# The gate and up gradients in DRAM: from rows of tokens to square blocks of one token tile and one f block

## The chip, the cores and the metric

The kernel runs on one core of a Trainium2 chip. The metric is the device time of one execution in microseconds (us). Of five runs of the kernel before, the median is 2046.41 us, the fastest 2044.51 and the slowest 2056.77.

The engines are named as the profile names them: PE multiplies matrices (PEld are its weight loads), DVE works on vectors, ACT on activations and copies, POOL and SP mostly issue DMAs here. PEq, SPq, ACTq and POOLq are the engines' instruction queues; each is in order, so an instruction that waits holds up all that stands behind it. The DMAs of all queues run on the same 16 DMA engines.

## The reference

The kernel computes a small network with its backward pass: a layer norm, a state-space convolution (A), a gated feed-forward block (B), their product, and the gradients of all inputs. There are L = 2048 tokens, D = 576 features, F = 4608 hidden features and N = 128 states. What matters here is the feed-forward block and its gradient:

```python
def _B_ref(x, w1, w3, w2):
    gate = jnp.einsum("bsd,df->bsf", x, w1)
    up = jnp.einsum("bsd,df->bsf", x, w3)
    h = _silu(gate) * up
    out = jnp.einsum("bsf,fd->bsd", h, w2)
    return out

xn = _layernorm(x)
s = _A_ref(xn, ...)
g = _silu(_B_ref(xn, w1, w3, w2))
out = x + s * g            # and jax.vjp of all this at grad_out
```

In the backward pass the gradient of `h` is formed first, then the gradients of gate and up (called gg and gu), all of shape 2048 x 4608. From these come the gradients of w1 and w3 (products with `xn` over the tokens) and the gradient of `xn` (products with w1 and w3 over f), which goes through the layer norm's own gradient into the gradient of x.

## The kernel before

Tokens are cut into LT = 16 tiles of 128, f into FT = 36 blocks of 128, and f also into 18 groups of FG = 256 (two blocks each). The kernel goes forward (up to some 800 us), then backward. In the backward part three streams of work interleave.

**The feed-forward gradient**, `phase6_group` (lines 1252 to 1281), once for each of 18 groups of f. `phase6_load` has loaded gate and up of this group from `GI_dram` into `gg_n` and `h_n`, and transposed rows of w2 into `w2T`. For four token tiles at a time PE forms the gradient of h (`ph`, line 1267), ACT copies it to `gh`, and DVE multiplies it into `gu_n` and `gg_n` (line 1273). Then `gu_n` and `gg_n`, each 128 tokens x 16 tiles x 256 f, are stored to `GU_dram` and `GG_dram` (line 1280) by four DMAs on SP's queue, and `phase6_grad13` (line 1314) forms the gradients of w1 and w3 from the same tiles on PE. `phase6_grad2` (line 1295) forms the gradient of w2.

**The convolution's gradient** (`ssm_bwd_conv`, mostly DVE) runs until about 1280 us; after it `param_quarter` (lines 1042 to 1075) loads transposed pieces of `Q_dram` into `qT` by SP's queue, and PE (line 1065) and DVE reduce them to the parameters' gradients, until about 1870. `phase5_final` then makes and stores the small parameter gradients (`gout`).

**The gradient of the input**, `phase6_inputs` (lines 1329 to 1363), once for each of 16 token tiles, from about 1650 to the end. `ggc` and `guc` (two buffers each) hold gg and gu of one token tile, transposed: f within a block on the partitions, then 36 blocks x 128 tokens. They are read from `GG_dram` and `GU_dram` by `nat_transpose` (line 1218), a DMA that transposes as it moves, on SP's queue. PE then makes 144 matmuls per token tile (line 1357) into two accumulators `px`, alternating between `ggc` and `guc` block by block, against transposed w1 and w3 kept in SBUF. DVE and ACT finish the tile through the layer norm's gradient (`ln_bwd_tile`).

The code names each step's due time with `self.at(us)`, which sets a priority; a planner orders each engine's queue by these priorities and by what is ready when it plays the program through at build time. So SP's queue holds stores of gg and gu, transposing loads of w2, w1, w3, Q, ggc and guc and plain loads, in one order fixed at build time, and instructions of the three streams stand between each other in it.

Before, `GG_dram` and `GU_dram` are [16 token tiles, 128 tokens, 4608 f]. A store takes eight token tiles (j = 0 or 1) of all 256 f of the group; in DRAM each token gets a run of 256 elements, 512 bytes. A load takes one token tile, [128 tokens, 4608 f], whose rows are 9,216 bytes apart.

Of the kernel before, what the change touches and what calls it, by code (L numbers as in the profile page):

```python
# [14 lines left out]
BF16 = mybir.dt.bfloat16  # L15
I32 = mybir.dt.int32
P = 128
# [42 lines left out]
class K:  # L60
# [1100 lines left out]
    def backward(self, T0, TG, TQ, TC, TX, gctx, mats):  # L1161
        nc, cfg = self.nc, self.cfg
        D, L, LT, F, FT = cfg.D, cfg.L, cfg.LT, cfg.F, cfg.FT
        self.GG_dram = self.dram.tile([LT, P, F], BF16, name="GG_dram")
        self.GU_dram = self.dram.tile([LT, P, F], BF16, name="GU_dram")
        self.GXN_dram = self.dram.tile([P, LT, D], FP32, name="GXN_dram")
        NG = F // self.FG
        T2 = T0 + TG * NG
        FA = 12
        pool = self.tc.tile_pool  # L1170
        PS = bass.MemoryType.PSUM
        with ExitStack() as out:
            ffn = ExitStack()
            wp = ffn.enter_context(pool(name="e_w", bufs=2))
            elp = ffn.enter_context(pool(name="e_el", bufs=3))
            gwp = ffn.enter_context(pool(name="e_gw", bufs=2))
            rowp = ffn.enter_context(pool(name="e_w2r", bufs=1))
            inp = ffn.enter_context(pool(name="e_in", bufs=2))
            self.at(T0 - TG)
            self.w2rows = [rowp.tile([P, cfg.DT * P], BF16, name=f"w2r{i}") for i in range(4)]  # L1180
            for w2r in self.w2rows:
                nc.gpsimd.memset(w2r[:, D:cfg.DT * P], 0.0)
            ps_h = ffn.enter_context(pool(name="e_ps_h", bufs=3, space=PS))
            ps_gw = ffn.enter_context(pool(name="e_ps_gw", bufs=2, space=PS))
            ps = out.enter_context(pool(name="b_ps", bufs=3, space=PS, side="right"))
            self.ssm_bwd_conv(T0, TQ, ps)
            mats.close()
            fix = out.enter_context(pool(name="b_fix", bufs=1, side="right"))
            S_all = fix.tile([P, 4, D], FP32, name="S_all")
            wA = out.enter_context(pool(name="x_wA", bufs=1, side="right"))  # L1190
            self.at(T2 - 150)
            wT = [self.load_wT(wA, 0, FA)]
            T1 = T0 + 4 * TQ
            self.ssm_bwd_params(T1, TC, S_all, ps)
            self.at(T1 + TC * D // 16)
            self.phase5_final(out, fix, S_all, ps)
            cur = self.phase6_load(0, T0 - TG, TG, wp, inp)
            for gi in range(NG):
                nxt = self.phase6_load(gi + 1, T0 + TG * gi, TG, wp, inp) if gi + 1 < NG else None
                self.at(T0 + TG * gi)  # L1200
                self.phase6_group(gi, cur, elp, gwp, ps_h, ps_gw)
                cur = nxt
            ffn.close()
            gctx.close()
            self.phase6_inputs(T2, TX, FA, wT)
# [46 lines left out]
    def phase6_group(self, gi, tiles, elp, gwp, ps_h, ps_gw):  # L1252
        nc, cfg = self.nc, self.cfg
        D, LT, FG = cfg.D, cfg.LT, self.FG
        nfull = D // P
        LH = LT // 2
        w2T, hn, gg, gu = tiles
        for s in range(LH // 2):
            gh = elp.tile([P, 2, 2, FG], BF16, name="gh6")
            ph = [ps_h.tile([P, 2, FG], FP32, name="ph") for _ in range(2)]  # L1260
            for k in range(2):
                for j in range(2):
                    tt = s * 4 + j * 2 + k
                    m, i = divmod(tt, self.cfg.KT)
                    steps = [(self.goT[m][:, c, i * P:(i + 1) * P], w2T[:, :, c, :]) for c in range(nfull + 1)]
                    for n, (lw, rh) in enumerate(steps):
                        nc.tensor.matmul(ph[j][:, k, :].rearrange("p (a f) -> p a f", f=P), lhsT=lw, rhs=rh, start=(n == 0),  # L1267
                                         stop=(n == nfull))
            for j in range(2):
                nc.scalar.copy(out=gh[:, j], in_=ph[j][:])  # L1270
            sl = slice(s * 4, s * 4 + 4)
            for t_ in (gu, gg):
                nc.vector.tensor_tensor(out=t_[:, sl], in0=gh[:].rearrange("p j t f -> p (j t) f"), in1=t_[:, sl],  # L1273
                                        op=ALU.mult)
            if s % 2 == 1:
                self.phase6_grad2(gi, s // 2, hn, gwp, ps_gw)
        for (dst, t_) in ((self.GU_dram, gu), (self.GG_dram, gg)):
            for j in range(2):
                ts = slice(j * LH, (j + 1) * LH)
                nc.sync.dma_start(out=dst[ts, :, gi * FG:(gi + 1) * FG].rearrange("t p f -> p t f"), in_=t_[:, ts, :])  # L1280
        self.phase6_grad13(gi, gg, gu, gwp, ps_gw)

    def phase6_grad2(self, gi, fl, hn, gwp, ps_gw):
# [45 lines left out]
    def phase6_inputs(self, T2, TX, FA, wT):  # L1329
        nc, cfg = self.nc, self.cfg  # L1330
        D, DT, L, LT, F, FT = cfg.D, cfg.DT, cfg.L, cfg.LT, cfg.F, cfg.FT
        aps = self.aps
        pieces = self.dpieces()
        with self.tc.tile_pool(name="x_wB", bufs=1) as wB, \
                self.tc.tile_pool(name="x_in", bufs=2) as inp, \
                self.tc.tile_pool(name="l_sb", bufs=2) as sb, self.tc.tile_pool(name="l_sm", bufs=4) as sm, \
                self.tc.tile_pool(name="x_ps", bufs=2, space=bass.MemoryType.PSUM) as ps:
            for i in range(LT):
                self.at(T2 + TX * i)
                if True:  # L1340
                    ggc = inp.tile([P, FT, P], BF16, name="ggc")
                    guc = inp.tile([P, FT, P], BF16, name="guc")
                    self.nat_transpose(ggc[:], self.GG_dram[i])
                    self.nat_transpose(guc[:], self.GU_dram[i])
                    if i == 0:
                        wT = wT + [self.load_wT(wB, FA, FT)]
                    px = [ps.tile([P, 512], FP32, name=f"px{pi_}") for pi_ in range(len(pieces))]
                    gx = sb.tile([P, D], FP32, name="gx7")
                    gxs = sb.tile([P, D], FP32, name="gxs7")
                    nc.scalar.dma_start(out=gxs[:], in_=self.GXN_dram[:, i, :])  # L1350
                    go_t = sb.tile([P, D], BF16, name="go7")
                    nc.scalar.dma_start(out=go_t[:], in_=aps["grad_out"].flatten_outer_dims()[i * P:(i + 1) * P, :])
                    for fi in range(FT):
                        part, f = (0, fi) if fi < FA else (1, fi - FA)
                        for ai, act in enumerate((ggc, guc)):
                            for pi_, (po, pw) in enumerate(pieces):
                                nc.tensor.matmul(px[pi_][:, 0:pw], lhsT=act[:, fi, :], rhs=wT[part][ai][:, f, po:po + pw],  # L1357
                                                 start=(fi == 0 and ai == 0), stop=(fi == FT - 1 and ai == 1))
                    for pi_, (po, pw) in enumerate(pieces):
                        nc.vector.tensor_tensor(out=gx[:, po:po + pw].rearrange("p (g d) -> p g d", g=4),  # L1360
                                                in0=px[pi_][:, 0:pw].rearrange("p (g d) -> p g d", g=4),
                                                in1=self.perm(gxs[:])[:, :, pi_, :], op=ALU.add)
                    self.ln_bwd_tile(sb, sm, gx, i, go_t)
# [119 lines left out]
```

## Time and profile before

| What | Value |
|---|---|
| Median of 5 runs | 2046.41 us |
| The profiled execution's own time | 2044.51 us |
| Its span, from the first to the last instruction | 2042.7 us |
| PE busy | 1754.6 us, 86% |
| DVE busy | 1284.5 us, 63% |
| ACT busy | 940.0 us, 46% |
| DMA queue of SP (q1) | 615,952 packets, 294.84 MB, 58.6% of 16 engines |
| GU_dram and GG_dram stores | 36 each of 512 KB, median 5.0 and 6.2 us from issue to landing |
| ggc and guc loads | 16 each, on SP's queue for 5.27 and 5.31 us (median), 8.8 and 8.6 us from issue to landing |

A row of a wait reads: engine and line that waited, the work that ended the wait, total us, how many times, the longest. A row of a timeline reads: start in us from the span's start, duration, engine, line, operation, output and input. The duration of a DMA's row on SPq is the time that its issue held the queue, not the transfer. A DMA view gives, for a stretch of time, the throughput in 40 equal slices, and for each queue the packets, megabytes and the time that its packets took as a share of 16 engines over that stretch. A windows row gives start:end, length, busy us (and instructions) of PE, PEld, DVE, ACT and POOL, then the clock granted to PE as a share of full speed, the DMA share and GB/s.

### The profile page before, as it was taken

Reading aid. Unit: us, or ns where it says so; the run is one execution under the profiler, and the core shown is the slowest. Engines: PE = TensorE matmul, PEld = TensorE weight load, DVE = VectorE, ACT = ScalarE, POOL = GpSimd, SP = SyncE. Lnnn points to the kernel's source line nnn. Section 1 sums busy time; section 2 is a strip of 40 time slices with the busy share of each in tenths; the row PEclk is TensorE's granted clock in tenths of the full one; section 3 lists DMA queues with packets and bytes.
Section 4 is the critical chain, followed back from the end, with each engine's and each line's share of the span. In section 5 each row is a group of like instructions: output and inputs, shape, how many; then the busy total and the mean of one; then the engine's idle time right before and its main releaser. Section 6 shows DMA issues by size and latency. Waiting matters only on the chain.

```text
span 2042.7 us, 39357 instructions
## 1 busy us (share of the span) xinstructions
PE 1754.6 (86%) x16104; PEld 1281.6 (63%) x16104; DVE 1284.5 (63%) x2646; ACT 940.0 (46%) x1512; POOL 273.0 (13%) x347
## 2 busy tenths in 40 slices
PE   3779999999699995999999999868888926889978
PEld 1444444443388874778888888657777815668756
DVE  9558888978287723696966979435465341445722
ACT  5658888887545534745445454334554200000000
POOL 4113333333322103000000000000000000000000
PEclk7889999999899997999999999979899957999989
DMA  4868999998956568465664646999999799999673
GB/s 130 279 269 304 365 375 376 368 358 316 306 138 179 141 142 261 113 195 179 188 203 127 208 124 204 195 236 223 233 229 237 151 217 217 234 198 200 125 160 87
DMA packets 681861, 448.92 MB, mean 220 GB/s; under 512 B 477136, under 2 KB 640848, under 8 KB 671952
## 3 DMA queue, kind: packets, MB, share of 16 engines
q1 hardware_dynamic: 615952, 294.84, 58.6%
q0 software_dynamic: 27952, 126.24, 17.3%
q10 hardware_dynamic: 37776, 25.32, 4.5%
q8 instruction: 126, 2.06, 0.4%
q14 instruction: 55, 0.45, 0.1%
HBM read 128.29 MB, written 206.88 MB: 164 GB/s over the span
## 4 chain that ended last, share of the span: by engine, by line
PE 31%; DVE 20%; DMA 11%; SPq 6%; ACT 3%; issue 2%; POOL 0%; ACTq 0%; DVEq 0%; POOLq 0%
PE px L1357 9%; PE pgw L1314 8%; SPq L1218 5%; PE po L873 4%; DMA qT<-Q_dram 3%; DVE cm_t L696 3%; PE ph L1267 3%; PE pgw L1295 2%; DVE cm_t L693 2%; DMA guc<-GU_dram 2%; DVE Z L694 2%; DVE Z L699 1%; DVE Z L698 1%; DMA gg_n<-GI_dram 1%; PE et_ps L715 1%
## 5 line engine op out<-in xcount | busy, mean ns | idle before, releaser
L808 PE MATMUL pgu<-wmB_w,xnT 128*128 128x512 bf16 x1152 | 284.8, 380 | 1.1 <-ACT E L447 1.1
L1357 PE MATMUL px<-wTB_w,guc 128*128 128x288 bf16 x1152 | 244.7, 294 | 42.4 <-DMA guc<-GU_dram 29.8
L1357 PE MATMUL px<-wTB_w,ggc 128*128 128x288 bf16 x1152 | 245.4, 294 | 30.5 <-DMA ggc<-GG_dram 12.9
L1314 PEld LDWEIGHTS <-xn_bf 128*128 128x128 bf16 x2304 | 226.0, 98 | 37.3 <-issue 9.5
L1070 DVE TENSOR_TENSOR pr_q<-et_ps,pz 128x512 f32<-128x512 f32 x144 | 93.9, 682 | 195.7 <-PE et_ps L1065 120.4
L1267 PE MATMUL ph<-w2T,goT 128*128 128x256 bf16 x1440 | 194.1, 287 | 1.9 <-DMA w2T<-w2r 1.0
L808 PEld LDWEIGHTS <-xnT 128*128 128x128 bf16 x1152 | 102.7, 97 | 124.1 <-issue 23.3
L1374 ACT ACTIVATE t<-gx 128x576 f32<-128x576 f32 x16 | 10.9, 683 | 355.7 <-DVE gx L1360 263.9
L1357 PEld LDWEIGHTS <-guc 128*128 128x128 bf16 x1152 | 114.9, 100 | 81.1 <-DMA guc<-GU_dram 34.8
L1295 PE MATMUL pgw<-go_o,h_n 128*128 128x288 bf16 x1152 | 157.4, 291 | 7.9 <-DVE h_n L1249 7.8
L1267 PEld LDWEIGHTS <-goT 128*128 128x128 bf16 x1440 | 143.5, 102 | 28.5 <-issue 2.0
L1357 PEld LDWEIGHTS <-ggc 128*128 128x128 bf16 x1152 | 114.9, 100 | 57.9 <-issue 12.3
L873 PE MATMUL po<-w2g,hc 128*128 128x288 bf16 x1152 | 148.3, 286 | 2.7 <-DMA hc<-H_dram 2.7
L1316 ACT CAST gw<-pgw 128x256 bf16<-128x256 f32 x144 | 53.5, 373 | 202.6 <-PE pgw L1314 195.3
L1295 PEld LDWEIGHTS <-h_n 128*128 128x128 bf16 x1152 | 113.2, 99 | 37.6 <-DVE h_n L1249 8.6
L1360 DVE TENSOR_TENSOR gx<-px,gxs 128x288 f32<-128x288 f32 x32 | 13.3, 451 | 195.9 <-PE px L1357 195.9
L1314 PE MATMUL pgw<-gg_n,xn_bf 128*128 128x256 bf16 x1152 | 131.1, 275 | 4.4 <-ACT gw L1316 4.4
L1314 PE MATMUL pgw<-gu_n,xn_bf 128*128 128x256 bf16 x1152 | 131.7, 272 | 2.5 <-DVE gu_n L1273 1.6
L873 PEld LDWEIGHTS <-hc 128*128 128x128 bf16 x1152 | 111.2, 98 | 30.2 <-DMA hc<-H_dram 3.2
L1270 ACT CAST gh<-ph 128x512 bf16<-128x512 f32 x144 | 80.4, 591 | 84.6 <-PE ph L1267 59.3
L813 ACT CAST gu_t<-pgu 128x1024 bf16<-128x1024 f32 x108 | 110.3, 1023 | 11.1 <-DMA GI_dram<-gu_t 11.1
L811 ACT ACTIVATE s_t<-pgu 128x512 bf16<-128x512 f32 x144 | 87.7, 611 | 39.5 <-PE pgu L810 38.7
(323 smaller groups left out, 3490.4 us busy)
## 6 DMA issues: line engine op xcount, KB each, us to landing
GI_dram<-gu_t POOLq DMA_DIRECT2D x72, 512.0 KB, 7.6
Q_dram<-q_k SPq DMA_DIRECT2D x36, 1024.0 KB, 6.9
E_dram<-E_k POOLq DMA_DIRECT2D x18, 1152.0 KB, 5.7
E_l<-E_dram SPq DMA_DIRECT2D x36, 576.0 KB, 8.4
H_dram<-h_t SPq DMA_DIRECT2D x72, 256.0 KB, 7.3
gg_n<-GI_dram POOLq DMA_DIRECT2D x18, 1024.0 KB, 5.8
h_n<-GI_dram POOLq DMA_DIRECT2D x18, 1024.0 KB, 8.5
GU_dram<-gu_n SPq DMA_DIRECT2D x36, 512.0 KB, 5.0
```

Source lines behind the costliest of these rows:

```text
L696: tt_(out=f(t2), in0=f(B)[:, :, ::-1], in1=Az.rearrange("p q k d -> p q (k d)")[:, :, None].to_broadcast([P, Q, 2, KT * Wq]), op=ALU.mult)
L808: nc.tensor.matmul(pgu[:, j], lhsT=xnT[:, c, ts], rhs=wm[w][:, c, :], start=(c == 0), stop=False)
L811: nc.scalar.activation(out=s_t[:, :, q, :], in_=pgu[:, 0].rearrange("p (g f) -> p g f", g=ng), func=ACT.Silu)
L813: cp(out=gu_t[:, :, :, q, :], in_=pgu[:].rearrange("p u (g f) -> p u g f", g=ng))
L873: nc.tensor.matmul(pos[k][:, pi_, 0:pw], lhsT=hcs[k][:, fi, :], rhs=w2[fi][:, po:po + pw], start=(fi == 0), stop=(fi == FT - 1))
L1070: nc.vector.tensor_tensor(out=pr[:, s].rearrange("p k r x -> p r k x"), in0=T[:], in1=pz[:, s:s + 2, h * 8:h * 8 + 8, :].rearrange("p r d ...
L1218: self.nc.sync.dma_start_transpose(out=dst, in_=src)
L1267: nc.tensor.matmul(ph[j][:, k, :].rearrange("p (a f) -> p a f", f=P), lhsT=lw, rhs=rh, start=(n == 0), stop=(n == nfull))
L1270: nc.scalar.copy(out=gh[:, j], in_=ph[j][:])
L1295: nc.tensor.matmul(pgw[pi_][:, 0:pw], lhsT=hn[:, tt, fl * P:(fl + 1) * P], rhs=go_o[:, tt, po:po + pw], start=(tt == 0), stop=(tt == LT - 1))
L1314: nc.tensor.matmul(pw_[:, 0:FG], lhsT=self.xn_bf[:, tt, c * P:(c + 1) * P], rhs=nat[:, tt, :], start=(tt == 0), stop=(tt == LT - 1))
L1357: nc.tensor.matmul(px[pi_][:, 0:pw], lhsT=act[:, fi, :], rhs=wT[part][ai][:, f, po:po + pw], start=(fi == 0 and ai == 0), stop=(fi == FT - ...
```

## The change

The two DRAM tensors become [16 token tiles, 36 f blocks, 128 tokens, 128 f]: for each token tile and each f block one block of 128 x 128 elements, 32 KB, that lies in one piece. Within a token tile the 36 blocks follow each other, so the whole tile is one piece of 1.18 MB.

The stores are split by f block instead of by halves of the tokens: still four DMAs of 512 KB a group on SP's queue, in the order GU, GU, GG, GG in the program, but each now carries one f block of all 16 token tiles, and the run of one token is 128 elements, 256 bytes.

The loads see their source as a matrix of 4,608 rows (36 blocks x 128 tokens) by 128 columns, with rows of 256 bytes that follow each other without a gap, instead of 128 rows by 4,608 columns. What arrives in `ggc` and `guc` is the same, and so is all that follows.

```diff
@@ backward
-        self.GG_dram = self.dram.tile([LT, P, F], BF16, name="GG_dram")
-        self.GU_dram = self.dram.tile([LT, P, F], BF16, name="GU_dram")
+        self.GG_dram = self.dram.tile([LT, FT, P, P], BF16, name="GG_dram")
+        self.GU_dram = self.dram.tile([LT, FT, P, P], BF16, name="GU_dram")
@@ phase6_group
         for (dst, t_) in ((self.GU_dram, gu), (self.GG_dram, gg)):
-            for j in range(2):
-                ts = slice(j * LH, (j + 1) * LH)
-                nc.sync.dma_start(out=dst[ts, :, gi * FG:(gi + 1) * FG].rearrange("t p f -> p t f"), in_=t_[:, ts, :])
+            for l in range(FG // P):
+                nc.sync.dma_start(out=dst[:, gi * FG // P + l].rearrange("t p f -> p t f"), in_=t_[:, :, l * P:(l + 1) * P])
         self.phase6_grad13(gi, gg, gu, gwp, ps_gw)
@@ phase6_inputs
-                    self.nat_transpose(ggc[:], self.GG_dram[i])
-                    self.nat_transpose(guc[:], self.GU_dram[i])
+                    self.nat_transpose(ggc[:].rearrange("p l t -> p (l t)"), self.GG_dram[i].rearrange("l t f -> (l t) f"))
+                    self.nat_transpose(guc[:].rearrange("p l t -> p (l t)"), self.GU_dram[i].rearrange("l t f -> (l t) f"))
```

## The prediction

> **What bounds the kernel now.** I read the whole-kernel page first, then the windows view, then who waited for whom in the two stretches where the changed tensors live, then SP's queue in order of time. The windows view (start:end, length, then busy us of each engine, granted clock, DMA share, GB/s) has these stretches:
>
> ```profile
> 820.00:1280.00 460.00, 433.90 (x4512) 370.98 (x4511) 369.58 (x770) 230.35 (x461) 21.54 (x40) 1.00 0.57 172
> 1280.00:1640.00 360.00, 297.78 (x3165) 251.33 (x3162) 177.91 (x256) 140.85 (x235) 10.72 (x20) 0.90 0.99 217
> 1800.00:1850.00 50.00, 42.19 (x418) 33.28 (x416) 21.20 (x35) 1.55 (x4) 0.00 (x0) 0.93 1.13 201
> ```
>
> The stores of the change fall in the first two stretches, the transposing loads from 1640 on. In the first, DMA is only 57% busy. In the other two it is full, so a change in what a DMA costs can reach the end of the kernel. What PE waits for, in 1280 to 1640 (first line) and in 1640 to the end (the others; columns are total us, times, longest):
>
> ```profile
> PE et_ps L1065 <- DMA qT<-Q_dram: 52.5, 7, 24.2
> ```
> ```profile
> PE px L1357 <- DMA guc<-GU_dram: 29.8, 6, 7.8
> PE px L1357 <- DMA wTB_w<-in_B_w_dram: 25.3, 4, 10.9
> PE px L1357 <- DMA ggc<-GG_dram: 12.9, 3, 8.3
> ```
>
> So 42.7 us of PE's waits, about 2% of the kernel, end with a transposing load of the changed tensors. They are what a faster load could win, and the end is not all theirs: the chain of waits has one unbroken piece of PE px L1357 from 1963.33, 72.30 us long. The last four token tiles run at PE's own pace of 18 us, with loads that take 11 us of SP's queue per tile.
>
> **The loads: 16 of ggc and 16 of guc.** Each moves 36 blocks of 128x128, before and after. One transposing load of the same shape stands alone in the trace: hc from H_dram, laid out like GG_dram before. This is the DMA view of 610.7 to 617.0:
>
> ```profile
> GB/s 0 0 0 104 0 0 0 0 5 78 111 128 138 179 215 232 293 293 291 291 286 289 293 289 291 291 289 289 289 289 294 289 291 286 289 293 293 350 273 181
> q1 hardware_dynamic: 4640, 1.18, 83.6%
> ```
>
> 4,640 packets for 1.18 MB are 4,608 of 256 bytes (one row of one block each) and 32 of 4 bytes. 83.6% of 16 engines for 6.3 us over 4,640 packets is 18.2 ns per packet; in the packet records themselves the 10th, 50th and 90th percentiles are all 18 ns. The rate while it runs is 290 GB/s, 4.07 us for the 1.18 MB. The question is whether contiguous source rows make the packets larger or quicker. Two rows speak against it. The w2T loads, whose source rows lie in SBUF and not in DRAM, have the same 18 ns median; so the stride of 9,216 bytes between DRAM rows is not what a packet waits for. And a block is still 128 rows of 256 bytes each, spread over 16 engines. No load in this trace has a contiguous source, so the cost is bounded from both sides. The Trainium skill, "DMA: Bandwidth & Descriptors", section "Latency and other measured facts", gives a DMA transpose 261 GB/s with a non-contiguous middle dimension and some 350-400 GB/s when contiguous. By that rule (375 taken, an estimate) a load takes 3.15 us, 0.92 less. SP issues 16 of them between 1702.6 and 1864, where its queue has hardly a gap, and two more at 1945.9 and 1952.1 in front of PE's last wait: 18 x 0.92 = 16.5 us won at most, 2028. But the trace has 290, not 261, for the strided form, and packets without a tail. I take 0 and keep -16.5. On the other side, 16 neighbouring rows read at once could meet in the same part of the memory; with nothing in the trace to size it I allow 0.6 us a load, 18 x 0.6 = +11.
>
> **The stores: 72 before, 72 after, 512 KB each.** Before, a store writes runs of 512 bytes (one token, 256 f); after, runs of 256 bytes: 2,048 packets in place of 1,024. The first fence is a GU and a GG store before, alone, in 950.5 to 955.6; the second the small parameter stores (gout, 256-byte rows, SBUF to DRAM as the new stores are) in 1886.2 to 1889.2:
>
> ```profile
> q1 hardware_dynamic: 2080, 1.05, 67.2%
> ```
> ```profile
> q10 hardware_dynamic: 225, 0.05, 9.0%
> ```
>
> 67.2% x 5.1 us x 16 / 2,080 = 26.4 ns for 512 bytes; 9.0% x 3 us x 16 / 225 = 19.2 ns for 256 bytes. Per engine a store costs 64 x 26.4 = 1.7 us (1.8 at 290 GB/s), after the change 128 x 19.2 = 2.46 us if packets don't overlap, and 1.8 us, no more than before, if they overlap as in the hc load. I take 2.46: +0.65 us a store, +2.6 us for the four of a group, 47 us of engine time in all. The skill speaks against the change here: the same page, section "Specifications", wants at least 512 bytes and says that below it the engine reads, modifies and writes. If that doubles a byte's price, a 256-byte packet costs 28 ns, a store 3.6 us, +7.2 us a group. The row says 19.2, and I go by the row; 7.2 stays as the upper end.
>
> **What covers it.** Groups 0 to 8 end before 1280, where DVE sets the pace and DMA is 57% busy. Exposed there is only DVE's wait for the landing of GXN_dram stores on the same queue (10.5 us in 4 waits): 1 us, estimated from that. From 1340 each group does the same; SP's queue in one of them:
>
> ```profile
> 1363.03 0.54 SPq L1280 DMA_DIRECT2D GU_dram<-gu_n  x1
> 1363.67 0.57 SPq L1280 DMA_DIRECT2D GG_dram<-gg_n  x1
> 1364.34 2.02 SPq L1280 DMA_DIRECT2D GU_dram<-gu_n  x1
> 1366.45 1.38 SPq L1280 DMA_DIRECT2D GG_dram<-gg_n  x1
> 1367.92 7.47 SPq L1218 DMA_TRANSPOSE w2T<-w2r  x1
> 1381.01 12.32 SPq L1218 DMA_TRANSPOSE qT<-Q_dram  x3
> ```
>
> The w2T load, 1.2 us elsewhere, holds SP for 7.47 because four stores are ahead of it on the engines. It ends at 1375.4, and the qT loads that PE waits for next are issued at 1381.0, when PE has freed their buffers after 16 us of grad13. So 5.6 us of cover. The other groups by the same reading have 4.4 (1419.2 to 1423.6), 7.1, 6.3, 5.5, and 14 in the last two. Against it stand the 2.6 us and up to 1.3 us from order: a store used to carry eight token tiles and the first could go once half of them were multiplied; a block column has all sixteen, so the first pair waits for the last multiplication (1363.0 against 1364.3 here). 3.9 us is under 4.4: nothing shows. If the cover were gone all seven groups would pay, 27 us. The one group without cover is that of 1300: there PE waits 24.2 us for qT, behind SP's stores and ten weight loads in a row (1312.6 to 1340.9). It pays 2.6. On SP, what stands behind a store that waits longer is w2T and qT, whose readers are ph (a group later) and et_ps; POOL's loads of gg_n and h_n have their own queue and share only the engines. The last store is issued at 1617.7 and lands in about 6 us; the first ggc load is issued at 1647.5, so the store's new shape delays no load.
>
> **Sum.** Loads 0, early groups +1, the 1300 group +2.6, later groups 0: +3.6 on the profiled execution's own 2044.5 (span 2042.7 and 1.8 around it) is 2048.1. The median of the runs is 1.9 above that execution; the forecast as a median is 2050.
>
> **Rivals.** First, contiguous reads are quicker (the skill's 350-400): 2028 on the profile, 2030 as a median. For it: 42.7 us of PE waits to take from, a DMA share above 1. Against it: 18 ns whether rows come from DRAM or SBUF. Second, slower: 256-byte writes are dear. The place is the burst at the end of a group, the cover 4.4 to 7.1 us. It begins to cost once the burst grows by 3 us (with the 1.3 of order), which is 0.75 us a store or 20 ns a packet, and it passes +10 at about 25 ns. At 28 ns: 7.2 + 1.3 = 8.5 us against covers of 5.6, 4.4, 7.1, 6.3, 5.5 loses 13.6, with 7.2 at 1300 and some 3 early: +24, 2070. If the packets were twice as slow as 19.2, 38 ns, the burst grows by 12.2: 8 x 5 groups and 12 at 1300, +55, 2100. Third, the order on SP's queue comes out differently, since the planner that lays the queues out sees other stores. Whether qT or guc stands first decides waits of 6.6 to 7.8 us (tiles 1, 4 and 6). Two or three such waits more or fewer: 2030 to 2072, more easily worse, since the due times were set for the old order; slow loads (+11) are put with it.
>
> **Chances.** The loads unchanged and the stores covered: 0.50, with its own range 2042 to 2058. Quicker loads 0.14. Dear stores 0.18. Another order or slower loads 0.18. Faster by over 0.5% (10 us, about what a measurement of this kernel can tell from no change): 0.11 of the second and 0.03 of the fourth, 0.14. Slower by over 0.5%: 0.17 of the third, 0.12 of the fourth, 0.06 of the first, 0.35. The rest, 0.51, within. The range leaves out the better half of the quick loads and the tail of the dear stores: 2033 to 2080.
>
> **What would show it.** In the profile after, one load of ggc alone should again have 4,608 packets of 256 bytes at 18 ns and hold SP for 4.5 to 5.3 us; GU and GG stores should have 2,048 packets at 18 to 20 ns; the w2T load behind a burst should end before the qT loads' buffers come free; PE's waits for guc and ggc should stay near 43 us. I am wrong if the load's packets change size or rate, if the wait of et_ps for qT grows by more than 5 us between 1340 and 1640, or if the order of ggc, guc and qT on SP's queue differs.

## The result and the profile after

Run side by side on one chip, the changed kernel takes 2067.05 us (median) and the kernel before 2055.58 us: a ratio of 1.0050, with a 95% interval of 1.0034 to 1.0066. The ratio leaves out executions in the chip's slower state, so it is not quite the ratio of the two medians. The forecast was +3.6 us, a ratio of 1.0018. What came is about +10 us, at the edge of what the prediction counted as no change, and on the slower side. On the 2046.41 us of the first five runs it is 2056.6, inside the range of 2033 to 2080. The profiled execution of the changed kernel takes 2064.16 us with a span of 2062.4, against 2044.51 and 2042.7 before. Lines of the file beyond the stores have moved up by one, so L1357 is now L1356, and so on.

The windows view of the changed kernel, in the same stretches, shifted by 20 us where the later start needs it (columns as before):

```profile
820.00:1280.00 460.00, 432.95 (x4472) 369.32 (x4471) 364.91 (x759) 224.63 (x456) 20.48 (x38) 0.99 0.59 170
1280.00:1660.00 380.00, 301.04 (x3217) 253.72 (x3214) 181.79 (x263) 143.58 (x238) 10.72 (x20) 0.90 1.02 207
1820.00:1870.00 50.00, 44.00 (x427) 34.25 (x423) 24.19 (x42) 2.02 (x6) 0.00 (x0) 0.93 1.05 208
```

The middle row has the loss. Its stretch was taken 20 us longer, and still PE is busy for only 301 us of it instead of 298, while the DMA engines move 207 GB/s where they moved 217, although they are busy for as large a share. (Counted from one point of the work to another, this stage takes 337.0 us instead of 321.8; the two rows stand under the table further down.) PE's waits in 1280 to 1658 of the changed kernel (engine, line and what ended the wait: total us, times, longest):

```profile
PE et_ps L1065 <- DMA qT<-Q_dram: 42.5, 7, 12.4
PE ph L1267 <- ACT gh L1270: 16.3, 3, 8.6
PE pgw L1313 <- ACT gw L1315: 12.4, 1, 12.4
```

and from 1658 to the end:

```profile
PE px L1356 <- DMA guc<-GU_dram: 29.7, 6, 7.9
PE px L1356 <- DMA wTB_w<-in_B_w_dram: 23.5, 4, 10.3
PE px L1356 <- DMA ggc<-GG_dram: 12.2, 3, 8.6
```

The wait on the transposing loads of the changed tensors is where it was: 41.9 us, 42.7 before. The wait for qT has even shrunk, from 52.5 to 42.5. What has grown is PE's waiting for ACT: 16.3 us for the copies `gh`, where there was none, and 12.4 for a copy `gw`, where it was 4.4. ACT in turn waits for this, first before (1280 to 1640), then after (1280 to 1658):

```profile
ACT L1244 <- DMA gg_n<-GI_dram: 15.2, 5, 5.0
```

```profile
ACT L1244 <- DMA gg_n<-GI_dram: 42.5, 6, 19.1
```

L1244 is the Silu at the head of a group's preparation. It reads gg_n, which POOL loads from GI_dram. So the loss sits two steps from anything that the diff touches. SP's queue around the worst of these waits, in the changed kernel:

```profile
1369.14 3.97 SPq L1218 DMA_TRANSPOSE wTB_w<-in_B_w_dram  x2
1373.22 2.53 SPq L1218 DMA_TRANSPOSE w2T<-w2r  x2
1375.85 2.73 SPq L1279 DMA_DIRECT2D GU_dram<-gu_n  x2
1378.69 9.88 SPq L1279 DMA_DIRECT2D GG_dram<-gg_n  x2
1388.66 22.10 SPq L1218 DMA_TRANSPOSE qT<-Q_dram  x3
```

This is the group that the prediction showed at 1363 (its grad13 starts at 1364.7 before, at 1371.6 now). Before, the first store was issued 1.6 us ahead of grad13 with one w2T load behind the stores. Now it is issued 4.2 us after grad13's start, because two weight loads and both w2T loads stand ahead of it, and the GG stores leave SP at 1388.57, 17.0 us after grad13's start. POOL's next load of gg_n, which overwrites the tile that these stores read, before and after:

```profile
1380.95 0.54 POOL L1239 DMA_DIRECT2D gg_n<-GI_dram  x1 [0.30 <-PE et_ps L1065]
```

```profile
1394.40 0.54 POOL L1239 DMA_DIRECT2D gg_n<-GI_dram  x1 [14.05 <-DVE pr_q L1070]
```

Before, it goes 0.3 us after PE's last multiplication with gg_n, after the change 6.8 us after it. The trace's semaphore records (the times at which a DMA reports that it has landed) tell what it waited for: the last GG store of the group landed at 1393.84, 0.6 us before this load went; before the change it had landed at 1378.61, 2.0 us before PE was done with the tile. (The bracket names DVE, which is not what this load waits for.) The late load then runs beside the three qT loads and lands 16.4 us after its issue instead of 7.9. ACT, in order of time, in the same two stretches (the bracket is the idle time before the row and what ended it):

```profile
1383.66 1.13 ACT L1270 CAST gh<-ph 128x512 bf16<-128x512 f32 x2 [2.57 <-PE ph L1267]
1388.93 1.28 ACT L1244 ACT_TABLE_LOAD   x1 [4.13 <-DMA gg_n<-GI_dram]
```

```profile
1390.62 1.13 ACT L1270 CAST gh<-ph 128x512 bf16<-128x512 f32 x2 [2.57 <-PE ph L1267]
1410.83 1.28 ACT L1244 ACT_TABLE_LOAD   x1 [19.08 <-DMA gg_n<-GI_dram]
1412.12 1.06 ACT L1244 ACTIVATE gu_n<-gg_n 128x1024 bf16<-128x1024 bf16 x1
1413.08 1.06 ACT L1270 CAST gh<-ph 128x512 bf16<-128x512 f32 x2
```

The next two copies of `gh` stand behind the Silu in ACT's queue, and PE cannot go on with `ph` until they have freed its accumulators: it waits 6.25 and 1.43 us there. (This Silu prepares the group that comes next, not the one whose `gh` waits behind it; a later place for it in ACT's queue was not tried.) That group takes 53.8 us from grad13 to the next grad13, and took 42.5.

From there to the grad13 of the last group PE idles 25.5 us, 23.1 before. The last stage, by the chain of waits of the changed kernel, ends in the same long piece of PE work as before (72.83 us, 72.30 before). The guc load in front of that piece takes 16.56 us to land in place of 11.18, and PE waits for it 7.58 us in place of 5.17:

```profile
1946.08 19.58 PE px L1356 x143
1965.87 16.56 DMA guc<-GU_dram
1982.48 72.83 PE px L1356 x573
```

The packets are as forecast. SP's queue (q1) carries them in the page's list of queues:

```profile
q1 hardware_dynamic: 689680, 294.84, 59.7%
```

It had 615,952. The difference, 73,728, is 72 stores times 1,024, so every new packet is a store's and the loads still have 4,608 of 256 bytes. A ggc load holds SP for 5.05 us in the median (5.27 before), a guc load for 5.42 (5.31). While the last guc load of the changed kernel runs alone, from 2029 to 2031.5, the DMA engines move 290 GB/s on the mean, as in the load from strided rows that the prediction showed (290). GG stores alone, in the DMA view of 824.5 to 827.7 of the changed kernel:

```profile
GB/s 221 224 214 211 221 224 214 211 221 218 208 186 160 157 173 186 237 291 282 211 214 208 211 221 221 214 214 221 221 214 211 224 218 214 218 221 221 214 214 221
q1 hardware_dynamic: 2705, 0.69, 84.0%
```

215 GB/s over 16 engines is one packet of 256 bytes per engine every 19.1 ns; the prediction had 19.2. The two are not the same measure: 19.2 was a packet's own time, from the busy share, and by that measure a packet takes 84.0% x 3.2 x 16 / 2,705 = 15.9 ns here, with gaps between the packets. The stores before ran at 289 GB/s in the view that it used. So a store went from 1.81 to 2.44 us and the burst of four from 7.3 to 9.8: +2.5 us, forecast +2.6.

### The profile page after: what moved, and what is told of

It reads as the page before. It is cut to its first block, busy times and chain, and to the rows that moved or that the text cites. A ratio compares the mean times of both kernels' runs of the same rounds, so it can differ in the third digit from the quotient of the medians.

```text
span 2062.4 us, 39328 instructions
## 1 busy us (share of the span) xinstructions
PE 1763.1 (85%) x16104; PEld 1285.7 (62%) x16104; DVE 1284.3 (62%) x2646; ACT 940.0 (46%) x1512; POOL 273.5 (13%) x347
## 5 line engine op out<-in xcount | busy, mean ns | idle before, releaser
L1356 PE MATMUL px<-wTB_w,guc 128*128 128x288 bf16 x1152 | 247.0, 296 | 41.7 <-DMA guc<-GU_dram 29.7
L1356 PE MATMUL px<-wTB_w,ggc 128*128 128x288 bf16 x1152 | 247.7, 296 | 28.8 <-DMA ggc<-GG_dram 12.2
L1356 PEld LDWEIGHTS <-guc 128*128 128x128 bf16 x1152 | 115.9, 101 | 82.0 <-DMA guc<-GU_dram 34.7
L1356 PEld LDWEIGHTS <-ggc 128*128 128x128 bf16 x1152 | 115.8, 101 | 56.5 <-issue 10.9
L1313 PE MATMUL pgw<-gg_n,xn_bf 128*128 128x256 bf16 x1152 | 130.7, 275 | 12.4 <-ACT gw L1315 12.4
L813 ACT CAST gu_t<-pgu 128x1024 bf16<-128x1024 f32 x108 | 110.2, 1022 | 10.5 <-DMA GI_dram<-gu_t 10.5
```

The costliest lines, as they stand in the source:

```text
L813: cp(out=gu_t[:, :, :, q, :], in_=pgu[:].rearrange("p u (g f) -> p u g f", g=ng))
L1313: nc.tensor.matmul(pw_[:, 0:FG], lhsT=self.xn_bf[:, tt, c * P:(c + 1) * P], rhs=nat[:, tt, :], start=(tt == 0), stop=(tt == LT - 1))
```

## The experiments

Theory at the start: the loss comes from the stores and from the order of the queues that the planner lays out with them. Rivals: the loads' share (a gain hidden inside a larger loss, or none); a loss from packets as such; a loss from leaving a favourable order; and chance meetings of POOL's loads with transposing loads. Three readings are compared over all kernels in a table further down.

### One side of the change alone

The loads alone: the old layout, read with one source row per 128 f, as the new loads are.

```diff
-self.nat_transpose(ggc[:], self.GG_dram[i])
+self.nat_transpose(ggc[:].rearrange("p l t -> p (l t)"),
+                   self.GG_dram[i].rearrange("t (l f) -> (t l) f", f=P))
 ... (guc the same)
```

> Stores as before; each load of ggc and guc reads the same 1.18 MB as 4,608 contiguous rows of 256 bytes, as after the change, so that their values are permuted and the gradient of the input is not the reference's. All five queues have the order of the kernel before. My theory (a load's packets stay 256 bytes at 18 ns, contiguous or not, so loads are worth nothing): ratio to before 0.998 to 1.002, ggc holds SP for 5.1 to 5.5 us in the median, PE's waits for ggc and guc 38 to 46 us. Rival (contiguous reads are quicker, cost hidden elsewhere): 0.99 to 0.995. Rival (the loads are what made the change slower): 1.004 to 1.007.

Measured: ratio 0.9981 (0.9958 to 1.0003), 2050.08 us. A ggc load holds SP for 5.01 us, and PE waits 31.7 us for guc and 12.0 for ggc, as before. The hold is a little under the 5.1 to 5.5 that was expected, the rest within. The interval allows a gain of 8.6 us at most; the 16.5 of the quick-load rival are excluded.

The stores alone: the new layout and stores, the loads written with the old shape of access over that memory.

```diff
-self.nat_transpose(guc[:].rearrange("p l t -> p (l t)"), self.GU_dram[i].rearrange("l t f -> (l t) f"))
+self.nat_transpose(guc[:], self.GU_dram[i].rearrange("l t f -> (l t) f")
+                                          .rearrange("(t l) f -> t (l f)", l=FT))
 ... (ggc the same)
```

It reads the rows of a tile in another order, so the values that reach px are not the gradients in their places.

> Stores and DRAM layout as after the change; the loads read the same bytes as 128 rows of 9,216 bytes, as before, so their values are permuted and the gradient of the input is not the reference's. All five queues have the order of the changed kernel. My theory (the whole loss is the stores and the order planned around them): ratio 1.003 to 1.007, the same as the changed kernel; the losses in its trace again lie before the first px matmul (between 820 and 1660 us). If the slow stretches of the changed kernel's one profile (gg_n landing after 16 us at 1394, qT holding SP 17 us at 1304) were chance, they are absent here or stand elsewhere. Rival (the loads): 1.000.

Measured: 1.0078 (1.0051 to 1.0105), 2069.97 us, a little above the 1.007 that was expected at most. The whole loss is on the stores' side.

### Packets and order, each in part

Old layout and runs of 512 bytes, but a store takes half of the partitions of all 16 token tiles, so that it too must wait for the last multiplication:

```diff
-ts = slice(j * LH, (j + 1) * LH)
-... out=dst[ts, :, gi * FG:(gi + 1) * FG] ..., in_=t_[:, ts, :]
+ps_ = slice(j * 64, (j + 1) * 64)
+... out=dst[:, ps_, gi * FG:(gi + 1) * FG] ..., in_=t_[ps_, :, :]
```

> Layout and loads as before and runs of 512 bytes; each tensor's store is split into two by halves of the partitions instead of by token tiles, so that, as after the change, each store waits for the last multiplication, and the planner lays the queues out anew (its order is neither that of before nor that of after). If the loss comes from the stores' later start: ratio 1.003 to 1.007 with packets unchanged. If it comes from the smaller packets (a burst longer by 4 x 0.7 to 0.9 us): 0.998 to 1.002. If any new order costs something: 1.002 to 1.01, with the loss at other places than in the changed kernel.

Measured: 1.0048 (1.0023 to 1.0073), 2064.88 us. By itself this looked as if order alone did it. But the DMA view of this kernel, 827.4 to 830.0, while its GG stores run alone, shows that the edit had slowed the stores as well:

```profile
GB/s 205 165 189 158 197 173 165 189 150 205 165 158 197 158 189 181 150 197 165 181 189 142 197 173 158 189 165 197 165 165 197 150 205 165 158 197 158 189 158 118
q1 hardware_dynamic: 885, 0.45, 77.6%
```

174 GB/s, less than the 256-byte stores. A store from 64 partitions takes 3.0 us, where one from 128 takes 1.8. The run does not separate order from slow stores; it is a second kind of slow store.

New layout, runs of 256 bytes, but a store takes half of the token tiles as before:

```diff
-for l in range(FG // P):
-    ... out=dst[:, gi * FG // P + l] ..., in_=t_[:, :, l * P:(l + 1) * P]
+for j in range(2):
+    ts = slice(j * LH, (j + 1) * LH)
+    ... out=dst[ts, gi * FG // P:(gi + 1) * FG // P] ..., in_=t_[:, ts, :] ...
```

> From the kernel before: stores split by halves of the token tiles as before, so each can start at the same time as before, but in runs of 256 bytes (a layout of group, token tile and block); the loads read 1.18 MB pieces of it as 128 rows of 9,216 bytes, so their values are permuted and the gradient of the input is not the reference's. The planner's order differs from before and after. If the packets cost the time: 1.003 to 1.007, and the stores' engine time 2.3 to 2.5 us each. If the later start costs it: 0.998 to 1.002. If it is the order on the queues: anything from 0.997 to 1.01, read from where its groups lose time.

Measured: 1.0079 (1.0053 to 1.0104), 2067.21 us. Up to the grad13 at 1366 it is level with the kernel before to 1.5 us; then it loses 10 us to the next. So the wait for all sixteen tiles is not needed for the loss. But slower stores are not the only thing left: in that group this kernel too has two weight loads ahead of its stores on SP, and the first store goes 1.9 us after grad13's start in place of 1.6 us ahead of it.

```profile
1364.08 3.90 SPq L1218 DMA_TRANSPOSE wTB_w<-in_B_w_dram  x2
1368.08 4.93 SPq L1280 DMA_DIRECT2D GU_dram<-gu_n  x2
```

### The reload of gg_n

First the changed kernel once more:

> The changed kernel once more, unchanged, to see which of its losses come back in another execution. Buffer theory (the reload of gg_n waits until the GG_dram stores of the same buffer have landed, and these land later now): the load of gg_n near 1394 is again issued 5 to 9 us after PE's last multiplication with gg_n, and the interval from the second half of grad13 at 1386 to the next is again 36 to 41 us (before: 28.5). Collision theory (a POOL load that meets transposing loads of qT on the engines is slow by chance): the slow landings (over 10 us) come back at other groups, and the interval may be anything from 28 to 41 us. Both: 2062 to 2070 us, ratio 1.003 to 1.008.

Measured: 1.0064 (1.0041 to 1.0087). gg_n's load near 1395 is again late, 7.2 us after PE's last use of the tile; from the last part of grad13 (line 1319) to the next group's grad13 it is 34.2 us (39.7 in the first profile, 28.5 in the kernel before). The place comes back, its price varies.

Then GG_dram written from gu_n, so that gg_n's reload has no store to wait for:

```diff
-for (dst, t_) in ((self.GU_dram, gu), (self.GG_dram, gg)):
+for (dst, t_) in ((self.GU_dram, gu), (self.GG_dram, gu)):
```

> The changed kernel, with GG_dram written from gu_n in place of gg_n: the same stores in the same order on SP, with the same packets; all other queues as they are. It leaves the true gate gradient out of GG_dram (out_1, which is made from it, is not the reference's). gg_n's reload then waits for PE alone. Buffer theory: every load of gg_n is issued within 2.5 us of the start of the second half of grad13 plus 8.7 (PE's end), the interval at 1386 falls from 39.7 to 29 to 33 us, and the time to 2053 to 2060, ratio 0.999 to 1.003. Packet theory (twice as many packets take engine time from whatever else runs): as the changed kernel, 2064 to 2070, ratio 1.004 to 1.008. Collision theory: the load is issued earlier and may meet other transposing loads; 2055 to 2070, with one to three landings over 10 us.

Measured: 1.0041 (1.0019 to 1.0062), 2064.37 us. POOL and ACT in the group in question:

```profile
1392.71 0.53 POOL L1239 DMA_DIRECT2D gg_n<-GI_dram  x1 [7.67 <-PE et_ps L1065]
```

```profile
ACT L1244 <- DMA GG_dram<-gu_n: 6.2, 1, 6.2
PE et_ps L1065 <- DMA qT<-Q_dram: 9.8, 1, 9.8
```

The load goes 0.3 us after PE's last multiplication with gg_n, in place of 6.8. That settles what it waited for: nothing but the tile that the store reads was changed. But the time hardly follows: 1.0041 is above the 0.999 to 1.003 that was expected if this reload were the whole loss. The Silu writes gu_n, so it now waits for the same stores through its other operand, 6.2 us here, and the qT loads stand behind the burst as before. The dependency was moved, not taken away. A third buffer for gg_n, 8 KB in each partition, should take it away; it was not tried.

Last, the GG stores written ahead of the GU stores:

```diff
-for (dst, t_) in ((self.GU_dram, gu), (self.GG_dram, gg)):
+for (dst, t_) in ((self.GG_dram, gg), (self.GU_dram, gu)):
```

> The changed kernel with the GG stores written ahead of the GU stores in the loop; on SP the order becomes GU, GG, GG, GU where it was GU, GU, GG, GG (in every group but the last few), all other queues are as they are. Buffer theory: the GG stores land one store (2.5 us of the engines) earlier, so gg_n's reload near 1394 is issued 2 to 4 us earlier and the time is 2 to 6 us under the changed kernel's, ratio 1.000 to 1.005. Packet theory: no difference, ratio 1.004 to 1.008. Collision theory: no difference in the mean.

Measured: 1.0062 (1.0035 to 1.0090), 2070.84 us. On SP the order became GU, GG, GG, GU. gg_n's load goes 3.9 us after PE's last use, in place of 6.8:

```profile
1397.33 0.53 POOL L1239 DMA_DIRECT2D gg_n<-GI_dram  x1 [11.21 <-DVE pr_q L1070]
```

The Silu waits 5.7 us in that group, in place of 19.1, and PE no longer waits for `gh` there. The group falls from 53.8 to 45.1 us. Yet in its profile the whole is no faster: it came into this group 12.7 us behind the kernel before (6.9 in the changed kernel), PE waits 7.6 us there for qT (5.9), and other groups have taken waits of their own (20.1 us late at 1597, 17 at the end of the stage). The place was repaired and the total stayed within its interval. By their totals both kernels lie where the rival of more packets as such had put them, 1.004 to 1.008: what happens at the reload is shown, that it makes up the whole loss is not.

> The kernel before with two edits: its transposing loads written with one source row per 128 f (as in loads_only), and the GG stores written ahead of the GU stores in the loop. SP's order changes in the stores and, from 1380 on, in what lies beside them; the other queues are as before. Buffer theory: gg_n's reload, which waits for PE alone before, gains nothing but is safer against late stores; 2046 to 2052, ratio 0.996 to 0.999, so at best a little under both kernels. Packet theory and collision theory: 2048 to 2054, ratio 0.997 to 1.000.

This is the kernel before with the edits of the loads run and of this one. Measured: 1.0000 (0.9975 to 1.0026). Which store goes first on SP costs nothing measurable where the stores are quick.

### Is it only the order that the planner lays?

All kernels with slow stores also have newly laid queues. So the due times of the groups were shifted, which lays new queues and touches no store:

```diff
-self.at(T0 + TG * gi)
+self.at(T0 + TG * gi - 3)      # or + 6
 self.phase6_group(gi, cur, elp, gwp, ps_h, ps_gw)
```

> The kernel before with the due time of each group of gate and up gradients 3 us earlier and nothing else: the same stores and loads, in queues that the planner lays out anew (on PE some 11,000 of 32,169 rows stand elsewhere, on DVE 900 of 2,370). Order theory (the order before is a favourable one, and a newly laid one costs about 0.5% whatever the stores are): ratio 1.003 to 1.008, 2062 to 2073 us. Store theory (the loss is in the new stores: later start, more packets, gg_n's reload behind them): 0.998 to 1.002, 2052 to 2061.

> The kernel before with the same due times 6 us later (PE some 4,700 rows elsewhere, DVE 470). Order theory: ratio 1.003 to 1.008. Store theory: 0.998 to 1.002; a due time so late may cost by itself, 1 to 3 us.

> The changed kernel with the due time of each group 3 us earlier (PE some 11,000 rows elsewhere than in the changed kernel). Order theory: the sum of the order's luck, anything from 0.998 to 1.008, and no worse than the same shift of the kernel before. Store theory: 1.003 to 1.008 again, 4 to 8 thousandths above the same shift of the kernel before.

> The changed kernel with the due times 6 us later. Order theory: anything from 0.998 to 1.010, and no worse than the same shift of the kernel before. Store theory: 1.004 to 1.010, 4 to 8 thousandths above the same shift of the kernel before.

Measured: before, 1.0009 (0.9982 to 1.0036) and 1.0006 (0.9982 to 1.0031); after, 1.0069 (1.0041 to 1.0098) and 1.0039 (1.0015 to 1.0063). These new queues alone cost nothing that can be measured, and the new stores cost 3 to 6 thousandths in three orders. The theory that any new order costs half a percent falls. An order that puts weight loads ahead of quick stores was in none of these kernels, so what such an order costs by itself stays untested. The shift by +6 may lessen the loss, but the intervals overlap.

### All kernels in one table

SP held: the sum of the rows of the 72 GU and GG stores on SP's queue. PE idle and Silu waits: from grad13 of the eighth group from the end to that of the last, one stretch in each kernel, with the same work (some 2,800 matmuls); idle is the length less PE's busy time, Silu is ACT's idle time just before L1244 there, whatever ended it.

| Kernel | Store | Ratio | SP held, us | PE idle, us | Silu waits, us |
|---|---|---|---|---|---|
| before | 512-byte runs, 8 tiles | 1 | 68 | 57.5 | 15.2 |
| loads only | the same | 0.9981 | 64 | 51.1 | 13.4 |
| loads, GG first | the same | 1.0000 | 65 | 60.7 | 12.1 |
| before, due -3 | the same | 1.0009 | 57 | 56.0 | 13.9 |
| before, due +6 | the same | 1.0006 | 60 | 52.2 | 11.1 |
| after | 256-byte runs, 16 tiles | 1.0050 | 171 | 72.5 | 40.1 |
| after, again | the same | 1.0064 | 174 | 61.4 | 30.5 |
| after, GG from gu_n | the same | 1.0041 | 170 | 67.4 | 30.7 |
| after, GG first | the same | 1.0062 | 181 | 66.9 | 25.4 |
| stores only | the same | 1.0078 | 182 | 72.8 | 49.8 |
| after, due -3 | the same | 1.0069 | 193 | 67.6 | 53.4 |
| after, due +6 | the same | 1.0039 | 173 | 61.9 | 51.2 |
| token halves | 256-byte runs, 8 tiles | 1.0079 | 119 | 69.7 | 43.9 |
| partition halves | 512-byte runs, 64 partitions | 1.0048 | 127 | 63.0 | 44.8 |

The two groups do not overlap in any column, though for PE's idle time the gap is narrow (60.7 against 61.4, with one profile of each kernel). The mean of PE's idle time is 55.5 us over the five with the old stores and 67.2 over the seven with the new ones: 11.7 us more. The mean of the ratios is 0.9999 and 1.0058, which is 12 us of 2055. The two agree, so this stretch accounts for most of the loss. (SP held overstates the difference in cost: before, part of the burst's time is in the row of the w2T load behind it, 7.47 us where it takes 1.2 elsewhere.) The rows that the two ends come from, for the kernel before and for the changed one:

```profile
1295.60:1617.40 321.80, 264.34 (x2803) 222.40 (x2801) 161.36 (x230) 125.37 (x208) 10.69 (x20) 0.89 1.01 220
```

```profile
1298.50:1635.50 337.00, 264.49 (x2802) 222.12 (x2801) 160.06 (x228) 125.17 (x208) 10.68 (x20) 0.89 1.03 207
```

PE's work is the same to 0.2 us and its clock the same; all 15 us are idle. None of the kernels tried is measurably faster than the kernel before.

What of the queues is the same in all seven: SP has weight loads and two w2T loads ahead of the stores in the group at about 1372. In the five with old stores the stores there follow one w2T load and no weight load. PE's idle time in that group is 4.7 to 5.8 us in the five and 7.6 to 13.6 in the seven. No run parts the stores' later place in the queue from their slower transfer: in every kernel here the two came together. For this group of the changed kernel the trace allows an estimate. Counted from grad13's start, the last GG store landed at 14.0 us before and at 22.2 after. Of these 8.3 us, 5.9 are the later issue of the first store (1.6 us ahead of grad13, then 4.2 behind it) and 2.4 the longer way from there to the last landing (15.6 us, then 18.0). PE is done with gg_n at 16.0. So slower transfers alone would have made the reload late by some 0.4 us; most of its lateness there is the place in the queue. Which later wait each kernel takes also differs from one profile to the next.

## Why the prediction was right, and where not

**Range and sum.** The result lies in the range, near the upper end of the first branch's own (2042 to 2058), but by the range's width: the sum of the terms, 3.6, is short by more than 6 us. None of the three signs of being wrong came: the load's packets are as they were, the wait for qT from 1340 on fell from 52.5 to 42.5 us, and ggc, guc and qT follow each other on SP as before. The loss took a way that none of them watched.

**The loads at 0**: right. Packets, hold on SP and PE's waits did not move, and loads alone give -0.19% (-0.42 to +0.03), -4 us. The estimate from the Trainium skill's figure for contiguous sources ("DMA: Bandwidth & Descriptors", "Latency and other measured facts"), -16.5 us, did not come: contiguous rows move at 290 GB/s like the strided ones, and going by the row was right.

**The price of a store**: right in size, +2.5 us for a burst of four alone against +2.6, but in part by luck: the packet itself takes 15.9 ns, not 19.2, and the gaps between packets make up the rest of 19.1. The same page's rule for writes under 512 bytes ("Specifications"), taken as twice the price of a byte, gives 28 ns by an estimate; no run shows that. So the rival of dear stores, which begins at 20 ns, is not what happened, though its place was the right one.

**Later groups covered**: nearly right in six of seven. From 1407 to 1640 PE waited 22.6 us for qT before, and 24.2 from 1425 to 1658 after. SP's burst in these groups ends 7 to 14 us after grad13's start, ahead of the 16 at which qT's buffers come free. The 1.3 us for the wait for all tiles was short: the stores start from 1.3 us ahead of grad13 to 2.5 us after it, where they started 0.1 to 3.7 us ahead, 2.3 us later on the mean; in this profile the cover still held. It is thin: in two further kernels with the new stores the burst of one such group left SP only after 18 and 19 us, and PE's idle time in these groups is 23.6 us on the mean of the five and 26.0 on that of the seven.

**The group at 1365**: here the sum failed. "3.9 us is under 4.4: nothing shows" kept SP's order as it was, with the stores ahead of all else at grad13's start. In the new order they start 5.9 us later there, not 1.3, behind 6.5 us of weight and w2T loads, and the cover is gone: the burst leaves SP 17.0 us after grad13's start, where qT's buffers come free after 16. Even so PE's wait for qT there hardly grew (5.75 us before, 5.94 after); the price came by the reload of gg_n. Idle time in this group: 5.8 us before, 13.6 after, 11 on the mean of the seven against 5 on that of the five. The prediction had such an order among its rivals, but looked for it between qT and guc and not between stores and weights.

**"POOL's loads of gg_n and h_n have their own queue and share only the engines"**: wrong, and the reason why the lateness reached PE by a way that no wait of before showed. gg_n's load overwrites the tile that the store reads. Before, the stores had landed by the time that PE was done with the tile, so the view put the wait down to PE. The store's landing was a second wait hidden under it, with 2.0 us to spare. After, it came last, and what followed is Silu, `gh`, `ph`.

**1300, +2.6**: PE's idle time from grad13 there to the next group's was 28.6 us before and 33.4 after, 26.7 and 30.3 on the two means: +3.6. Size about right, way wrong: the wait for qT shrank from 24.2 to 12.4, and waits for ACT grew from 4.4 to 21.0 (12.4 and 8.6).

**Early groups, +1**: between 938 and 1296 PE's idle time went from 21.2 to 22.9, and to 23.2 to 24.3 in four further kernels with new stores, due times as they were: +2 to +3. The reason given for the +1 did not hold: DVE's wait for the GXN_dram stores was 10.5 us before and is 8.3 to 11.1 in the five profiles with new stores. The cause is open.

The forecast's terms add up to 3.6; the runs have about 2 early, 3.6 at 1300, 6 in place of 0 at 1365, and 2 in the groups after it, some 14 us of PE's idle time on the means, and 12 us by the ratios.

## What to carry to other kernels

When a store gets slower, look at who overwrites its source: a buffer's reload waits for its reader's transfer as well as for its compute, and a view of waits shows only the one that ended last. A cover that was measured in one order of the queues holds only as long as that order does; where a planner lays the queues, ask what it will put ahead of an operation that becomes ready later. A layout that helps one side of a transfer should be charged for the other: here the loads gained nothing from contiguous blocks, and the stores paid for the halved runs.

## What the runs showed of the hardware

- A store from SBUF to DRAM of 512 KB ran at 289 GB/s in 512-byte runs from 128 partitions, 215 in 256-byte runs, and 174 in 512-byte runs from 64 partitions. The last had not been expected; why 64 partitions are slower no run shows.
- Where a large copy ran beside transposing loads, both could become very slow. In the changed kernel POOL's h_n load at 1298.5 landed 20.1 us after issue, and the two qT loads beside it held SP for 5.30 and 17.00 us; in the packet records from 1303 to the landing, 917 packets of 256 bytes took 114 ns on the mean, with a median still at 18, and those of 8,192 bytes up to 7.8 us. In the kernel with GG stored from gu_n the last packet of the load at the same place came after 6.8 us, and that of the next load, gg_n's, after 19.5. So it is not tied to one place, and what sets it off is open.
- The granted clock of PE moved single profiles by more than half of the effect. The same 3,522 matmuls in the kernel before and in the second profile of the changed kernel (columns as before, the clock third from the end):

```profile
938.40:1295.60 357.20, 336.00 (x3522) 288.10 (x3522) 284.46 (x599) 179.59 (x361) 15.65 (x30) 1.00 0.58 171
938.40:1305.40 367.00, 342.68 (x3522) 292.91 (x3522) 283.35 (x590) 180.15 (x361) 15.60 (x30) 0.97 0.60 169
```

At a clock of 0.97 PE is busy for 6.7 us longer, and only 3.1 of the 9.8 us between the two are idle time. That is why the table compares PE's idle time and not the spans.
